# A planned attention and two-layer MLP kernel: more buffers at the start of the first batch, fewer warm-up matmuls, and the second batch's k and q sums moved from accumulating DMAs to VectorE

## The chip, the cores and the metric

One NeuronCore of one Trainium2 chip runs the whole program. The metric is the time of the program on the device in microseconds (us). It is the median of three runs; one further run, made with the hardware profiler, gives the trace.

## The reference, cut to what matters

Attention over 4 batches, 8 heads, 576 positions and 64 channels, then two feed-forward layers over 2304 tokens (512 to 2048 to 512 features). Attention is a sum of two parts: one on k, q and v averaged over groups of four positions, one local with a band of seven positions.

```python
q_d = q.reshape(B, H, Sd, factor, D).mean(axis=3)      # factor = 4, Sd = 144
k_d = k.reshape(B, H, Sd, factor, D).mean(axis=3)
v_d = v.reshape(B, H, Sd, factor, D).mean(axis=3)
out_up = np.repeat(sm_attn(q_d, k_d, v_d), factor, axis=2)
mask = np.abs(pos[:, None] - pos[None, :]) < factor
scores = np.where(mask, scale * np.matmul(q, k.transpose(0, 1, 3, 2)), -1e9)
x = out_up + softmax(scores) @ v                       # then heads beside each other: [2304, 512]
h = x @ moe_w_in;  x = (h * sigmoid(h)) @ moe_w_out
h = x @ moe2_w_in; g = P(h) / (Q(h) + 1e-6);  out = g @ moe2_w_out
```

## The kernel before

All matrix products of the two layers are made of three products each of high and low parts (fp32r), so a layer step is 24 matmuls: 12 for the first product (`h`, L807) and 12 for the second (`o`, L821). The first layer walks over five blocks of tokens (480 or 384) and 16 slices of the hidden width, 80 steps in all. The first block takes 8 steps, the second block 16, then the first block's other 8, then the rest.

The order of the work is not written out by hand. `Plan` (L94) keeps a list of jobs; each has a cost in ns for every engine that may do it (P is TensorE, V VectorE, A ScalarE, G GpSimd, D the SyncE DMA queue), jobs that must be done before it, and slots of rings (buffers) that it takes and gives back. `run` (L122) goes through the planned time and gives each job to an engine; `settle` (L112) repeats it and keeps the best. The result is one fixed order of instructions for each engine, and each engine's queue runs in that order. A job with `port` that V or G may do goes to the first free one of "VG" (L194), and such jobs do not overlap in the plan.

One attention job chain per batch `b`:

- `L` loads k and q of a third of the positions into a `kq` buffer (ring of 4). `v` and `V` load v.
- Sums of four positions: for batch 0 the jobs `R` make them on VectorE from the loaded `kq` (L408), and the jobs `p` make those of v on GpSimd or VectorE (L424, L426, L427). For the later batches the jobs `K` and `Q` load four slices with DMAs, three of them accumulating DMAs that GpSimd issues (L437, L444).
- Averaged part, two halves `m`: scores `s` (L471), maximum `m`, exponent `e` (ACT, L487), sum `u`, normalising `n` (L496, one job of 864 columns), transposes `t` (L505), copies `c`, product `o` (L519), copy `U` to `up`.
- Local part, six chunks `c` of 96 tokens: scores `S` (L572, L581), `M` (L587), `E` (L597), `U` (L602), `N` (L606), transposes `T` (L617), copy `C`, product `O` (L637), then `A` adds the two parts into `xs` (L644, ring of 2), `H` copies the high part, `X` subtracts it for the low part (L659).

Chunks 0 to 4 of batch 0 make the first block of tokens, so the first `h` step waits for these five. Weights are converted on the chip: each slice of a weight matrix is one `piece` of seven jobs on ACT, VectorE and GpSimd (L719 to L743), ahead of the step that uses it.

While TensorE has nothing to do it is kept busy with matmuls on a constant (`warm`, L287). They write the PSUM tile `wps`, which has the tag `h` and so one of the two buffers of the `h` steps; a tile keeps its buffer up to its last use in the program. `warm(20)` stands in front, and gaps in the plan are filled up to a planned time of `HEAD + 15000` ns (L1011 to L1015).

Of the kernel before, what the change touches and what calls it, by code (L numbers as in the profile page):

```python
# [21 lines left out]
CH = 96  # L22
# [29 lines left out]
EARLY = 50000.0  # L52
ROUNDS = 6
WARM0 = 20
WARM_SHARE = 0.8

# [37 lines left out]
class Plan:  # L94
# [27 lines left out]
    def run(self, when):  # L122
# [26 lines left out]
        while events:  # L149
# [18 lines left out]
            while again:  # L168
                again = False
                for j in pool:  # L170
# [22 lines left out]
                    if "G" in j.cost and "V" in j.cost and j.port:  # L193
                        best = next((e for e in "VG" if free[e] <= t), None)  # L194
                        if best is None:
                            continue
# [58 lines left out]
def tile_kernel(ctx, tc, kq, kqs, vp, vw_in, moe_w_in, moe_w_out, moe2_w_in, moe2_w_out, moe2_a, moe2_b, out):  # L255
# [119 lines left out]
    def attention(b):  # L375
# [22 lines left out]
        if b == 0:  # L398
            for t in range(3):
                for w in range(2):  # L400
                    def sm(e, t=t, w=w):
                        if w == 0:
                            o = kd[:, :, SUB * t:SUB * t + SUB]
                            i = kqt[t][:, :KT * KW].rearrange("p (g s) -> p g s", g=KT)[:, :, HALO:HALO + TH]
                        else:
                            o = qd[:, :KT * SD].rearrange("p (g s) -> p g s", g=KT)[:, :, SUB * t:SUB * t + SUB]
                            i = kqt[t][:, KT * KW:KT * (KW + TH)].rearrange("p (g s) -> p g s", g=KT)
                        nc.vector.tensor_reduce(out=o, in_=i.rearrange("p g (j r) -> p g j r", r=4), axis=AX.X, op=ALU.add)  # L408
                    sums.append(plan.add(f"R{b}{t}{w}", FAR, {"V": v_ns(768)}, sm, after=[loads[t]] + sums[:1],
                                         take=[] if sums else [kdu], give=[kqu[t]]))  # L410
            for i in range(2):
                for hf in range(2):
# [16 lines left out]
                    vs.append(plan.add(f"p{b}{i}{hf}", FAR, {"G": 2050, "V": 1950}, pv,  # L429
                                       after=[l] + vs[:1], take=[] if vs else [vdu], give=[u]))  # L430
        else:
# [14 lines left out]
            for f, u, o, n, m in ((ks, kdu, sums, "K", 128 * 4608), (vsum, vdu, vs, "Q", HS * 4096)):  # L446
                j = None
                for r in range(4):
                    j = plan.add(f"{n}{b}{r}", FAR, {"G": 1000} if r else {"D": 60}, lambda e, f=f, r=r: f(e, r),
                                 after=[j] if j else takes[n], take=[] if j else [u], size=m, margin=500 if r else 0)  # L450
                    if r == 0:
                        takes[n] = [j]
                o.append(j)
        if b == 0:
            takes.update(K=sums[:1], Q=vs[:1])

# [3 lines left out]
        for m in range(2):  # L460
# [34 lines left out]
            def no(e, x=x):  # L495
                eng(e).tensor_tensor(out=x["e"][:, :, :SD], in0=x["e"][:, :, :SD],  # L496
                                     in1=x["r"].unsqueeze(2).to_broadcast([128, 6, SD]), op=ALU.mult)
# [34 lines left out]
            jn = plan.add(f"n{b}{m}", d0, {"V": v_ns(864), "G": 130 + 1.9 * 864}, no, after=[ju], port=True)  # L532
            pc, pt_ = [], []
            for e_, u in ((0, p1_), (1, p2)):
                jt = plan.add(f"t{b}{m}{e_}", d0, {"P": 500}, lambda e, tr=tr, e_=e_, u=u: tr(e, e_=e_, u=u),
                              after=[jn] + pt_[:1], take=[u] + ([pt] if e_ == 0 else []), give=[eu], margin=MARGIN if b else MARGIN0)
# [9 lines left out]
        for c in range(NCH):  # L546
# [7 lines left out]
            wn = NF - 3 + c // 2  # L554
            if b == 0 and c in (3, 4):
                pt = v0u.setdefault("PT", Unit("w8"))
# [84 lines left out]
            def ad(e, x=x, c=c):  # L641
                x["x"] = at.tile([128, KT, CH], F32, tag="xs", name="xs", bufs=2)
# [18 lines left out]
            if i == 0:  # L661
# [14 lines left out]
            jo = plan.add(f"O{b}{c}", d0, {"P": 700}, pv, after=[jc, jl] + ups, take=[pO, xu], give=[pt, vu],  # L676
                          margin=MARGIN if b else MARGIN0)
            ja = plan.add(f"A{b}{c}", d0, {"V": 2 * v_ns(192)}, ad, after=[jo], give=[pO, upu])
# [331 lines left out]
    busy = 0.0  # L1010
# [173 lines left out]
```

## Time and profile before

| what | value |
| --- | --- |
| three runs, median | 925.39 us |
| three runs, range | 923.1 to 926.2 us |
| profiled execution, its own time | 925.37 us |
| profiled execution, span from first to last instruction | 923.6 us |
| TensorE matmul busy | 906.2 us (98%) |
| TensorE weight loads busy | 762.3 us (83%) |
| VectorE busy | 711.4 us (77%) |
| ScalarE busy | 606.8 us (66%) |
| GpSimd busy | 333.2 us (36%) |
| mean granted TensorE clock | 0.996 |

The profiled execution took as long as the median of the runs, and 1.8 us of its time lie outside the span. Times of rows below count from the start of the span. The chain of work that ended last runs through TensorE for 91% of the span. An average says little here: attention of the first batch, attention beside the first layer, and the two layers alone follow each other, and only the first 112 us hold waits of TensorE.

### The profile page before, as it was taken

How to read it: one execution, taken by the hardware profiler on the slowest of the kernel's cores; microseconds unless marked ns; L12 is line 12 of the kernel's file. 1: busy time of each engine (PE TensorE's matmuls, PEld its weight loads, DVE VectorE, ACT ScalarE, POOL GpSimd, SP SyncE). 2: the span in 40 equal slices, each digit the busy share in tenths (PEclk: the TensorE clock that was granted, in tenths of full speed). 3: DMA queues.
4: the chain of work that ended last, by engine and by line, in shares of the span. 5: the costliest groups of instructions: out<-in, count | busy, mean ns of one | idle time of the engine just before them, and what ended most of it. 6: DMA issues, size and time to landing. Idle time of an engine off the chain costs nothing.

```text
span 923.6 us, 16216 instructions
## 1 busy us (share of the span) xinstructions
PE 906.2 (98%) x6212; PEld 762.3 (83%) x6212; DVE 711.4 (77%) x1060; ACT 606.8 (66%) x1224; POOL 333.2 (36%) x279
## 2 busy tenths in 40 slices
PE   8988999999999999999999999999999999999997
PEld 6766788877887778878899988888888888999996
DVE  6979876996557876785332399998998999799995
ACT  4957655786446764674322488877877777787874
POOL 4534240142022410121000155655555555455553
PEclk9989999999999999999999999999999999999999
DMA  9878997779789777779685091002001000200000
GB/s 282 287 217 247 277 282 279 251 268 301 220 269 294 238 276 276 268 245 363 213 288 210 5 392 48 1 1 92 1 1 48 33 1 1 80 1 0 35 1 35
DMA packets 48042, 153.03 MB, mean 166 GB/s; under 512 B 5244, under 2 KB 10492, under 8 KB 47964
## 3 DMA queue, kind: packets, MB, share of 16 engines
q1 hardware_dynamic: 44972, 143.03, 44.1%
q0 software_dynamic: 2704, 8.95, 5.4%
q8 instruction: 49, 0.80, 0.4%
q14 instruction: 29, 0.24, 0.1%
q10 hardware_dynamic: 288, 0.00, 0.0%
HBM read 116.38 MB, written 35.59 MB: 165 GB/s over the span
## 4 chain that ended last, share of the span: by engine, by line
PE 91%; DVE 4%; ACT 3%; issue 1%; POOL 0%; ACTq 0%; DVEq 0%; POOLq 0%
PE hps L807 43%; PE acc L1054 21%; PE acc L821 21%; PE wps L289 1%; PE pair L637 1%; PE pair L581 1%; PE pair L519 1%; ACT E L597 1%; PE pair L617 1%; DVE cw L735 1%; ACT cr L723 0%; DVE cr L732 0%; ACT PT L332 0%; DVE cw L728 0%; PE pair L471 0%
## 5 line engine op out<-in xcount | busy, mean ns | idle before, releaser
L807 PE MATMUL hps<-xh,w 128*128 128x480 f32 (+1 forms) x640 | 226.0, 381 | 3.6 <-DVE th L973 3.0
L821 PE MATMUL acc<-gh,wo 128*128 128x480 f32 (+1 forms) x640 | 222.8, 376 | 0.0
L807 PE MATMUL hps<-x2h,wi 128*128 128x512 f32 (+1 forms) x640 | 196.4, 368 | 0.0
L894 POOL TENSOR_TENSOR u<-u,ah 128x512 f32<-128x512 f32 (+1 forms) x80 | 96.0, 1200 | 262.7 <-ACT u L892 261.1
L1054 PE MATMUL acc<-wo,gh 128*128 128x512 f32 x576 | 178.0, 390 | 0.0
L807 PEld LDWEIGHTS hps<-xh,w 128*128 128x128 f32 x640 | 121.1, 189 | 22.5 <-DVE th L973 3.8
L821 PEld LDWEIGHTS acc<-gh,wo 128*128 128x128 f32 x640 | 119.8, 188 | 17.4 <-issue 1.8
L807 PEld LDWEIGHTS hps<-x2h,wi 128*128 128x128 f32 x640 | 118.8, 188 | 16.3
L1085 POOL TENSOR_TENSOR gl<-p,gh 128x512 fp32r<-128x512 f32 (+1 forms) x80 | 121.2, 1515 | 11.6 <-issue 8.9
L1054 PEld LDWEIGHTS acc<-wo,gh 128*128 128x128 f32 x576 | 107.6, 188 | 20.9
L807 PE MATMUL hps<-xl,w 128*128 128x480 f32 (+1 forms) x320 | 120.0, 375 | 1.1 <-DVE xl L659 1.0
L821 PE MATMUL acc<-gl,wo 128*128 128x480 f32 (+1 forms) x320 | 118.6, 371 | 0.4 <-POOL gl L982 0.4
L807 PE MATMUL hps<-x2l,wi 128*128 128x512 f32 (+1 forms) x320 | 117.7, 368 | 0.0
L1054 PE MATMUL acc<-wo,gl 128*128 128x512 f32 x288 | 112.7, 391 | 0.0
L970 ACT ACTIVATE th<-hps 128x480 f32<-128x480 f32 (+1 forms) x80 | 44.5, 557 | 101.7 <-PE hps L807 100.8
L973 DVE SCALAR_TENSOR_TENSOR th<-th,hps 128x480 f32<-128x480 f32 (+1 forms) x80 | 50.4, 631 | 78.9 <-ACT th L970 78.5
L1077 DVE SCALAR_TENSOR_TENSOR u<-u,r 128x512 f32<-128x512 f32 (+1 forms) x80 | 100.1, 1252 | 2.8
L1070 ACT ACTIVATE r<-u,cst 128x512 f32<-128x512 f32 (+1 forms) x80 | 54.5, 682 | 52.7 <-POOL u L894 52.7
L1076 DVE SCALAR_TENSOR_TENSOR u<-u,r 128x512 f32<-128x512 f32 (+1 forms) x80 | 82.7, 1034 | 0.5 <-ACT r L1071 0.5
L732 POOL TENSOR_TENSOR cr<-cw,cr 128x512 int32<-128x512 int32 x22 | 30.9, 1407 | 135.0 <-DVE cw L728 86.2
L891 DVE TENSOR_TENSOR p<-p,hps 128x512 f32<-128x512 f32 (+1 forms) x80 | 50.5, 631 | 31.5 <-ACT p L890 31.3
L332 ACT ACTIVATE gh<-th 128x480 fp32r<-128x480 f32 (+1 forms) x80 | 47.4, 592 | 31.8 <-DVE th L973 28.5
(123 smaller groups left out, 1485.4 us busy)
## 6 DMA issues: line engine op xcount, KB each, us to landing
wo<-wos SPq DMA_DIRECT2D x64, 512.0 KB, 5.8
raw<-moe_w_in SPq DMA_DIRECT2D x32, 512.0 KB, 5.0
raw<-moe_w_out SPq DMA_DIRECT2D x32, 512.0 KB, 5.9
w2s<-cvo SPq DMA_DIRECT2D x32, 512.0 KB, 5.2
kq<-kq SPq DMA_DIRECT2D x12, 788.0 KB, 7.5
wos<-wo SPq DMA_DIRECT2D x16, 512.0 KB, 3.1
wi<-w2s SPq DMA_DIRECT2D x16, 512.0 KB, 6.6
wo<-w2s SPq DMA_DIRECT2D x16, 512.0 KB, 9.7
```

The lines of the kernel that those rows point to most:

```text
L332: nc.scalar.activation(out, in_, AF.Copy, scale=scale)
L807: nc.tensor.matmul(hps[:, :n], lhsT=wi[:, i, 128 * g:128 * g + 128], rhs=(a, b)[s][:, g, :n], start=(m == 0), stop=(m == len(mms) - 1))
L821: nc.tensor.matmul(acc_t[p][g // 2][:, g % 2, :n], lhsT=wo[:, i, 128 * g:128 * g + 128], rhs=s_[:, :n], start=(f == f0 and m % 3 == 0), st ...
L891: nc.vector.tensor_tensor(out=p, in0=p, in1=hps, op=ALU.mult)
L894: nc.gpsimd.tensor_tensor(out=u, in0=u, in1=ah, op=ALU.mult)
L970: nc.scalar.activation(x["t"][:, :n], x["h"][:, :n], AF.Tanh, scale=0.5)
L973: nc.vector.scalar_tensor_tensor(out=x["t"][:, :n], in0=x["t"][:, :n], scalar=1.0, in1=x["h"][:, :n], op0=ALU.add, op1=ALU.mult)
L1054: nc.tensor.matmul(acc2[j][c], lhsT=a[:, 128 * c:128 * c + 128], rhs=wo[:, i, :], start=(f == 0 and m % 3 == 0), stop=(f == NF - 1 and m % ...
L1070: nc.scalar.activation(r, u, AF.Ln, scale=2.0 ** -64, bias=cst[:, 0:1])
L1076: nc.vector.scalar_tensor_tensor(out=u, in0=u, scalar=1.000001, in1=r, op0=ALU.add, op1=ALU.mult)
L1077: nc.vector.scalar_tensor_tensor(out=u, in0=u, scalar=-2.0, in1=r, op0=ALU.add, op1=ALU.mult)
L1085: nc.gpsimd.tensor_tensor(out=gl2[k_][:, :n], in0=p, in1=gh2[k_][:, :n], op=ALU.subtract)
```

## The change

Seven edits. (1) The four chunks 2 to 5 of batch 0 get `xs` buffers in the weight slots w9 and w10, one slot for two chunks; the product `O` of chunks 3 and 5 takes no slot of its own and follows the product before it. (2) The sums of v in batch 0 may run on GpSimd alone. (3) A `port` job that GpSimd or VectorE may do prefers GpSimd when another job that only VectorE can do, and that is no `port` job, is ready. (4) `n` is two jobs of 432 columns each, and the transposes of a half wait for their own half. (5) Batch 1's sums of k and q are made like batch 0's, by the six `R` jobs on VectorE from the loaded `kq`; its `K` jobs and their four DMAs are gone. (6) The take-over of the sum buffers from batch to batch follows this. (7) The fill-up with warm-up matmuls counts from 3500 ns on.

```diff
+SUMS_V = 2
+COLD = 3500.0
@@ Plan.run
                     if "G" in j.cost and "V" in j.cost and j.port:
-                        best = next((e for e in "VG" if free[e] <= t), None)
+                        rest = any(x.ready <= t and not x.port and x.only() == "V" for x in pool)
+                        best = next((e for e in ("GV" if rest else "VG") if free[e] <= t), None)
@@ attention
-        if b == 0:
+        if b < SUMS_V:
             for t in range(3):
                 for w in range(2):
...
+        if b == 0:
             for i in range(2):
...
-                    vs.append(plan.add(f"p{b}{i}{hf}", FAR, {"G": 2050, "V": 1950}, pv,
+                    vs.append(plan.add(f"p{b}{i}{hf}", FAR, {"G": 2050}, pv,
...
+                if n == "K" and b < SUMS_V:
+                    continue
...
-                                 after=[j] if j else takes[n], take=[] if j else [u], size=m, margin=500 if r else 0)
+                                 after=[j] if j else takes[n] if b > 1 or n == "Q" else [], take=[] if j else [u], size=m, margin=500 if r else 0)
...
+        elif b < SUMS_V:
+            takes.update(K=sums[:1])
...
-                eng(e).tensor_tensor(out=x["e"][:, :, :SD], in0=x["e"][:, :, :SD],
-                                     in1=x["r"].unsqueeze(2).to_broadcast([128, 6, SD]), op=ALU.mult)
+                i = slice(3 * e_, 3 * e_ + 3)
+                eng(e).tensor_tensor(out=x["e"][:, i, :SD], in0=x["e"][:, i, :SD],
+                                     in1=x["r"][:, i].unsqueeze(2).to_broadcast([128, 3, SD]), op=ALU.mult)
...
-            jn = plan.add(f"n{b}{m}", d0, {"V": v_ns(864), "G": 130 + 1.9 * 864}, no, after=[ju], port=True)
+            jn = [plan.add(f"n{b}{m}{e_}", d0, {"V": v_ns(432), "G": 130 + 1.9 * 432}, lambda e, no=no, e_=e_: no(e, e_=e_),
+                           after=[ju], port=True) for e_ in range(2)]
...
-                              after=[jn] + pt_[:1], take=[u] + ([pt] if e_ == 0 else []), give=[eu], margin=MARGIN if b else MARGIN0)
+                              after=[jn[e_]] + pt_[:1], take=[u] + ([pt] if e_ == 0 else []), give=[eu], margin=MARGIN if b else MARGIN0)
...
+            if b == 0 and c >= 2:
+                xu = v0u.setdefault(("xs", c // 2), Unit(f"w{NF - 8 + c // 2}"))
...
+                if b == 0 and c >= 2:
+                    if c % 2 == 0:
+                        v0t["xs", c // 2] = wp.tile([128, 2, KT, CH], F32, tag=f"w{NF - 8 + c // 2}", name="xs2")
+                    x["x"] = v0t["xs", c // 2][:, c % 2]
...
-            jo = plan.add(f"O{b}{c}", d0, {"P": 700}, pv, after=[jc, jl] + ups, take=[pO, xu], give=[pt, vu],
+            jo = plan.add(f"O{b}{c}", d0, {"P": 700}, pv, after=[jc, jl] + ups + (o2 if b == 0 and c in (3, 5) else []), take=[pO] + ([] if b == 0 and c in (3, 5) else [xu]), give=[pt, vu],
                           margin=MARGIN if b else MARGIN0)
+            o2 = [jo]
@@ the fill-up
-    busy = 0.0
+    busy = COLD
```

## Rows read from the trace of the kernel before

**Rows 1.** Windows: start:end, length, busy us (count) per engine, PEclk, DMA share, GB/s
```profile
14.00:29.00 15.00, 12.32 (x251) 9.44 (x248) 13.91 (x25) 12.94 (x54) 12.79 (x12) 1.00 1.02 364
29.00:45.00 16.00, 14.83 (x393) 11.31 (x387) 15.20 (x36) 15.06 (x46) 7.56 (x7) 1.00 0.81 242
45.00:60.00 15.00, 11.02 (x84) 8.44 (x77) 10.42 (x22) 6.80 (x19) 7.03 (x7) 0.77 0.95 263
56.00:60.00 4.00, 4.00 (x18) 2.85 (x18) 0.18 (x1) 0.76 (x2) 1.27 (x2) 0.50 1.05 242
...
60.00:112.00 52.00, 48.95 (x480) 37.19 (x478) 47.03 (x82) 37.78 (x84) 16.83 (x14) 1.00 0.81 242
```
**Rows 2.** Waits of TensorE from 100 us to the end: total, times, longest
```profile
PE hps L807 <- ACT xh L332: 0.4, 1, 0.4
```
**Rows 3.** Timeline: start us, length us, engine, line, operation, count, [idle before <-releaser]; the start
```profile
1.06 8.71 PE L289 MATMUL wps<-wz 128*128 128x256 bf16 x59 [1.06 <-DVE wz L284]
6.73 1.81 DVE L408 TENSOR_REDUCE kqd<-kq 128x192 f32<-128x768 f32 x2 [2.39 <-DMA kq<-kq]
10.63 0.61 DVE L587 TENSOR_REDUCE n<-pair 128x8 f32<-128x432 f32 x1 [2.09 <-PE pair L581]
```
**Rows 4.** Timeline from the first exponent to the averaged part's result
```profile
19.14 0.21 ACT L593 ACTIVATE n<-n 128x8 f32<-128x8 f32 x1 [1.71 <-DVE n L587]
20.23 1.98 DVE L424 TENSOR_REDUCE vd<-vst 72x256 f32<-72x1024 f32 x1
25.22 3.39 POOL L496 TENSOR_TENSOR EE<-EE,r 128x864 f32<-128x864 f32 x2 [0.21 <-ACT EE L487]
34.69 0.41 ACT L332 ACTIVATE up<-pair 128x288 f32<-128x288 f32 x1
```
**Rows 5.** Timeline from the first local product to the first layer's first step
```profile
35.34 0.68 PE L637 MATMUL pair<-PT,vw 54*64 54x48 f32 x32
40.11 0.61 DVE L644 TENSOR_TENSOR xs<-acc,up 128x192 f32<-128x192 f32 x2
42.89 1.03 DVE L659 TENSOR_TENSOR xl<-xs,xh 128x384 fp32r<-128x384 f32 x2
45.77 1.52 DVE L732 CUSTOM_DVE_ANT_0 cr<-cw,cr 128x1024 uint16<-128x1024 uint16 x1
48.34 0.48 PE L807 MATMUL hps<-xl,w 128*128 128x480 f32 x1 [0.97 <-DVE xl L659]
```
**Rows 6.** Timeline of TensorE in the second step and after it
```profile
54.01 0.77 PE L807 MATMUL hps<-xh,w 128*128 128x480 f32 x1 [3.01 <-DVE th L973]
57.37 1.00 PE L807 MATMUL hps<-xh,w 128*128 128x480 f32 x2
59.70 1.39 PE L289 MATMUL wps<-wz 128*128 128x256 bf16 x10
63.24 0.59 PE L807 MATMUL hps<-xh,w 128*128 128x480 f32 x2
```
**Rows 7.** Groups by line: count, busy us, mean ns, idle before: the sums, and their DMAs' issue
```profile
L408 DVE TENSOR_REDUCE kqd<-kq 128x192 f32<-128x768 f32 x6 | 5.4, 945 | 2.4 <-DMA kq<-kq 2.4
L437 POOL DMA_DIRECT2D kqd<-kqs x9 | 8.8, 974 | 0.7 <-DMA kqd<-kqs 0.7
```
**Rows 8.** Timeline: VectorE's idle time behind the second step
```profile
59.82 0.65 DVE L973 SCALAR_TENSOR_TENSOR th<-th,hps 128x480 f32<-128x480 f32 x1 [4.34 <-ACT th L970]
```
**Rows 9.** Timeline: VectorE beside GpSimd
```profile
60.39 0.68 DVE L743 TENSOR_TENSOR w<-cw,w 128x512 fp32r<-128x512 f32 x1
66.84 1.30 POOL L743 TENSOR_TENSOR wo<-cw,wo 128x512 fp32r<-128x512 f32 x1 [9.57 <-ACT wo L332]
67.36 1.33 DVE L743 TENSOR_TENSOR w<-cw,w 128x512 fp32r<-128x512 f32 x1
70.17 0.61 DVE L602 TENSOR_REDUCE r<-E 128x8 f32<-128x440 f32 x1
70.20 1.29 POOL L732 TENSOR_TENSOR cr<-cw,cr 128x512 int32<-128x512 int32 x1 [2.06 <-ACT E L597]
```

More of the change, by code (lines that the diff above doesn't have):

```diff
@@ L493, in su, with no @@
                 nc.vector.reciprocal(out=x["r"], in_=x["r"])
-            def no(e, x=x):
-                eng(e).tensor_tensor(out=x["e"][:, :, :SD], in0=x["e"][:, :, :SD],
-                                     in1=x["r"].unsqueeze(2).to_broadcast([128, 6, SD]), op=ALU.mult)
+            def no(e, x=x, e_=0):
+                i = slice(3 * e_, 3 * e_ + 3)
+                eng(e).tensor_tensor(out=x["e"][:, i, :SD], in0=x["e"][:, i, :SD],
+                                     in1=x["r"][:, i].unsqueeze(2).to_broadcast([128, 3, SD]), op=ALU.mult)
             def tr(e, x=x, e_=0, u=None):
@@ L641, in ad @@
             def ad(e, x=x, c=c):
-                x["x"] = at.tile([128, KT, CH], F32, tag="xs", name="xs", bufs=2)
+                if b == 0 and c >= 2:
+                    if c % 2 == 0:
+                        v0t["xs", c // 2] = wp.tile([128, 2, KT, CH], F32, tag=f"w{NF - 8 + c // 2}", name="xs2")
+                    x["x"] = v0t["xs", c // 2][:, c % 2]
+                else:
+                    x["x"] = at.tile([128, KT, CH], F32, tag="xs", name="xs", bufs=2)
                 for a in range(2):
```

## The prediction

> **What bounds the kernel now.** I read the busy times by stretch first, then TensorE's waits, then the head instruction by instruction. From 60 us on TensorE is busy for 48.95 of 52 us [rows 1], and from 100 us to the end it waits 0.4 us in all [rows 2]. Everything behind 112 us is a queue of TensorE work that the change leaves as long as it is; what moves is when that queue starts and what TensorE loses before it is dense. The head has three stages. Up to 10.6 us TensorE runs 59 warm-up matmuls [rows 3]. From there to 34.7 us ScalarE is the tight engine: 12.94 of 15 us, then 15.06 of 16 [rows 1], with one idle stretch of 1.71 us [rows 4]. From 35.3 to 48.3 us the chunks are added up and split, while VectorE is busy 15.20 of 16 us [rows 1, 5]. [...]
>
> **The change part by part.**
>
> *Warm-up.* 59 matmuls are 20 plus 39, so the plan's first TensorE job starts between 39 x 109 / 0.8 = 5314 and 5450 ns. Counting from 3500 leaves (1814 to 1950) x 0.8 / 109 = 13 or 14, in all 33 or 34. At 8.71 / 59 = 0.148 us each they end at 1.06 + 34 x 0.148 = 6.1 us, a little later if the first ones are the slow ones, and still before the first k and q land, which let VectorE start at 6.73 [rows 3]. The first scores then start at about 6.8 instead of behind the warm-up at 9.8, and end before VectorE has done its two sums at 8.54. The first maximum moves from 10.63 to about 8.55: the 2.09 us that VectorE waited for TensorE [rows 3]. Nothing is late in its place before the second and third loads; those were not waited for before, so at 2 us less they cost between 0 and 2 us. I take 0.
>
> *From there to `up`.* ScalarE is nearly full, so a gain here is at most the start's 2.1 plus its idle 1.71 [rows 4]. The v sum of 1.98 us on VectorE goes; its GpSimd twin is planned at 2.05 in the kernel's text, on an engine that is busy 12.79 of 15 us [rows 1, 4]. VectorE's gain lies under ScalarE's work, and GpSimd's 2.05 lies ahead of the two normalisations, 3.39 us back to back [rows 4]. Halved, the first transposes need a quarter of these, 0.85 us, instead of half, which gives back 0.85. Bounds for this stage: 0.5 us (2.1 less 2.05, plus 0.45 of the half) and 3.8. I take 2.5, near the shift of the start, because ScalarE's row says that little else can be pulled ahead.
>
> *Buffers.* From the first local product at 35.34 to the matmul that reads the last low part at 48.34 are 13.0 us [rows 5]. With two `xs` buffers the third chunk's sum starts only at 40.11. Without that wait VectorE needs 5 x 0.61 us of sums (two instructions took 0.61) and 5 x 0.51 of subtractions (two took 1.03) [rows 5], 5.6 us; with the first product, one high-part copy and the hand-overs, an estimate of three times the product's 0.68 [rows 5], 2.0 us, it is a floor of 7.6. The gain is 5.4 if nothing else runs between, and 0 if weight conversions such as the 1.52 us one at 45.77 still fill the stretch. I take 3.0, a little over half: the wait itself goes, but the second step's weights are still converted here. The slots w9 and w10 are asked for again only by slices 9 and 10, whose step stands behind 17 others, so that cover is long; if it failed, a load of weights would wait, not TensorE.
>
> *k and q sums of batch 1.* Six reductions of 0.945 us, 5.67 us, are added to VectorE, and four DMAs of 576 KB fall away, three with a GpSimd issue of 0.97 us each [rows 7]: 2.36 MB, at the 242 to 364 GB/s of the head [rows 1] 6 to 10 us of transfer time. Batch 1's third `kq` load has to come earlier for it, 0.79 MB on the SyncE queue, with its turn before weight loads. Cover on VectorE: 4.34 us idle behind the second step [rows 8] and about 5 of 52 us after 60 [rows 1]. Queued behind the sums are batch 1's maxima and weight conversions, and TensorE waits for both. The price is 0 to 5.7 us; I take 1.0, since the idle time is 9 us, most of it right where the sums fall, and GpSimd takes over some conversions.
>
> *GpSimd first.* A job moved costs GpSimd about 1.3 us where VectorE needs 0.68 [rows 9]; GpSimd is free two thirds of the time after 60 us [rows 1]. It pays when VectorE meanwhile does what it was chosen for. A reduction beside a GpSimd job took 0.61 us, no longer than alone; a two-input conversion took 1.33 instead of 0.68 [rows 9]. So the pairing that the rule looks for is the good one, but order on the chip drifts from the plan. Between -3 and +5 us; I take -1.0, nearer to the reduction's row, because the six new sums are such reductions.
>
> [...]
>
> *The second step.* It waits for the first step's activation on VectorE, although the ring has two buffers, because warm-up matmuls still run at 59.70 and hold one [rows 6]. [...] The change touches neither; I take 0, bounds -5.4 and +5.4 (a step less or a step more).
>
> Sum: -2.5 - 3.0 + 1.0 - 1.0 = -5.5 us. The profiled execution took 925.37 us, 1.8 of it outside the span of 923.6, and equals the median of 925.39; so 920 us.
>
> **The rivals.**
>
> *One bank for longer (no change).* The limit of the warm-up is a planned time, 49 us. If the plan starts the first layer earlier, more steps lie before that limit, and a gap of 0.14 us in the plan is enough for a warm-up that holds the buffer. One more step that waits for its forerunner's activation costs 3.0 + 2.4 = 5.4 us: 920 + 5.4 = 925. For it: a planned start 3 us earlier is half a step. Against it: other TensorE work can fill such a wait, and the plan has a gap only where weights are late.
>
> *VectorE becomes the bound (slower).* Place: 45 to 112 us, where VectorE is busy 57.4 of 67 us [rows 1]; 9.6 idle. The sums take 5.7. If ten jobs that moved to GpSimd each stretch a conversion by 0.65 us (1.33 less 0.68), 6.5 more; together 12.2 against 9.6. Two more us are lost because the head's 5.5 us earlier start shortens the stretch for the same conversions: that eats the head's gain and leaves 12.2 - 9.6 + 2 = 4.6 us on top: 930. It decides once more than about six moved jobs overlap conversions. Against: moved jobs also take 0.68 each off VectorE, 6.8 for ten.
>
> *The head's gains add up and the second step's wait goes too (more gain).* All upper bounds, with the sums at 1: 2.1 + 1.7 + 5.4 + 5.4 - 1 = 13.6: 912.
>
> *The change doesn't do what it says.* If weights set the first steps, an earlier first block only waits longer: 924 to 926, told with the first rival.
>
> **How the numbers follow.** The forecast (gain of 3 to 9 us) has 0.54, the double gain 0.09, no change by the first or the last rival 0.21, slower 0.16. About 0.3%, 2.8 us, is what a measurement of this kernel can tell from no change: faster is below 922.6. Faster 0.63, same 0.21, slower 0.16. The forecast's own range is 916 to 922.5. The range for 8 in 10 is 913 to 929: it takes in the unchanged case and the near half of the slower one, and leaves out the far ends, about 0.14.
>
> **What would show it.** In the changed profile: 33 or 34 warm-up matmuls in front and the first scores near 6.8; the first maximum near 8.5; `up` near 32; the third chunk's sum right behind the second; the first low-part matmul near 43; the second step's wait and clock as before; the six sums between 25 and 70 us at 0.94 each; TensorE dense by 106. I am wrong if the first layer starts near 43 but TensorE then waits for weights or batch 1's maxima (the sums or GpSimd), if steps wait for the activation of the one before more than once (the bank), or if `up` stays near 35 (GpSimd ahead of the normalisations).

## The result and the profile after

The changed kernel takes 936.85 us (median of four runs) against 924.92 us of the kernel before: ratio 1.0107, 95% interval 1.0076 to 1.0137. It is slower by 12 us by the medians, against a forecast of 920.0 and a range of 913 to 929. The ratio takes in all four runs: three took 936.7 to 937.2 us and one 928.66. The profiled execution took 936.97 us with a span of 935.2, 11.6 more than before. The second layer starts 10.2 us later than before (529.08 instead of 518.84 us), so nearly all of the loss lies in front of it. Lines have moved: L293 is the old L289, L412 the old L408, L480 the old L471, L506 the old L496, L662 the old L644, L762 the old L743, L826 and L840 the old L807 and L821.

Windows of the changed kernel: start:end, length, busy us (count) of PE, PEld, DVE, ACT, POOL, then PEclk, DMA share, GB/s.

```profile
29.00:45.00 16.00, 14.84 (x281) 11.71 (x284) 10.35 (x23) 8.06 (x17) 6.19 (x6) 0.50 0.58 210
45.00:60.00 15.00, 14.08 (x178) 10.93 (x174) 13.22 (x22) 12.44 (x43) 8.33 (x7) 0.93 0.61 196
60.00:112.00 52.00, 45.73 (x473) 34.53 (x472) 44.01 (x85) 35.20 (x81) 17.93 (x15) 0.87 0.72 224
...
27.00:47.00 20.00, 18.37 (x346) 14.30 (x350) 13.40 (x27) 10.78 (x26) 6.19 (x6) 0.50 0.65 242
```

Against [rows 1] three things differ. From 29 to 45 us the granted clock is 0.50 where it was 1.00: TensorE is as busy as before (14.84 and 14.83 us) with 281 matmuls instead of 393, and ScalarE and VectorE, which wait for it (3.1 us for L529 and 5.1 for L650), are idle for half and a third of the stretch. The last window shows the whole of it, 20 us at 0.50. From 45 to 112 us VectorE is busy 57.2 of 67 us; before it was 57.4 (the six sums lie ahead of this stretch). And from 60 to 112 us TensorE does a little less than before, at a mean clock of 0.87.

Where TensorE's time went can be read from four more windows, from the start to the first matmul of the second layer: the kernel before and the changed one, then TensorE's warm-up matmuls alone in both.

```profile
0.00:518.84 518.84, 506.61 (x4364) 420.70 (x4365) 355.82 (x641) 298.29 (x709) 119.28 (x119) 0.99 0.80 260
0.00:529.08 529.08, 513.02 (x4338) 426.06 (x4339) 366.16 (x650) 296.49 (x707) 122.10 (x124) 0.97 0.75 251
...
0.00:518.84 518.84, 25.15 (x180) 0.99 0.80 260
0.00:529.08 529.08, 22.81 (x154) 0.97 0.75 251
```

Both kernels run the same 4,184 matmuls of their own there. Without the warm-ups these keep TensorE busy for 481.5 us before and 490.2 in the changed kernel, 8.7 us longer, while idle time and warm-ups together, the time in which TensorE waits, grow by 1.5 us only (37.4 to 38.9). So most of the loss in front of the second layer is the same work taking longer. The granted clock is at 0.50 from 26.7 to 47.2, from 67.7 to 77.9 and from 84.8 to 88.2 us, 34 us in all; before it was so for 6.8 us (53.2 to 60.0).

Timeline of the changed kernel: start us, length us, engine, line, operation, count, [idle before <-releaser].

```profile
1.06 6.30 PE L293 MATMUL wps<-wz 128*128 128x256 bf16 x33 [1.06 <-DVE wz L288]
7.20 0.35 PE L585 MATMUL pair<-bands,ident 128*128 128x216 bf16 x2
8.50 0.60 DVE L600 TENSOR_REDUCE n<-pair 128x8 f32<-128x432 f32 x1
...
23.34 4.50 DVE L506 TENSOR_TENSOR EE<-EE,r 128x432 f32<-128x432 f32 x2
23.36 1.77 POOL L506 TENSOR_TENSOR EE<-EE,r 128x432 f32<-128x432 f32 x2
25.09 1.77 POOL L619 TENSOR_TENSOR E<-E,r 128x432 f32<-128x432 f32 x2
27.47 0.70 PE L515 MATMUL pair<-ident,EE 48*72 48x48 f32 x12 [2.49 <-DVE EE L506]
35.12 0.41 ACT L336 ACTIVATE up<-acc 128x288 f32<-128x288 f32 x1 [1.63 <-PE acc L529]
38.95 0.62 DVE L662 TENSOR_TENSOR xs<-acc,up 128x192 f32<-128x192 f32 x2 [0.16 <-PE acc L650]
39.49 0.94 DVE L412 TENSOR_REDUCE kqd<-kq 128x192 f32<-128x768 f32 x1
48.50 0.47 PE L826 MATMUL hps<-xh,w 128*128 128x480 f32 x1
52.84 0.96 PE L480 MATMUL pair<-kqd 64*64 64x144 f32 x24
58.37 0.97 PE L480 MATMUL pair<-kqd 64*64 64x144 f32 x24 [0.59 <-ACT EE L496]
70.71 0.69 DVE L762 TENSOR_TENSOR w<-cw,w 128x512 fp32r<-128x512 f32 x1
73.47 0.77 PE L826 MATMUL hps<-xh,w 128*128 128x480 f32 x1
```

Read it from above. The start does what it should: 33 warm-ups, first maximum at 8.50 instead of 10.63 [rows 3]. At 23.3 us four GpSimd jobs lie beside two VectorE normalisations, which take 4.50 us; TensorE waits 2.49 us for them, and from 26.7 us on its clock is low. `up` is complete at 35.5 us, 0.4 later than before [rows 4]. The sums into `xs` follow each other with only a k sum between, so the buffers are there, but they start at 38 us. The last rows are another change: batch 1's scores of the averaged part (L480), which ran at 73.0 and 77.8 us before, now run at 52.8 and 58.4, and the last weight conversion in front of the third step (L762) ends only at 71.4 us, where the one at 60.39 ended at 61.1 before [rows 9]. The third step starts at 73.47 instead of 62.81. In the kernel before (timeline):

```profile
62.81 0.38 PE L807 MATMUL hps<-xh,w 128*128 128x480 f32 x1
73.00 0.97 PE L471 MATMUL pair<-kqd 64*64 64x144 f32 x24
```

The weights were late before these scores ran. The second step's conversion ended at 44.5 us before and at 57.2 in the changed kernel, and the third step's weights, the third load of `moe_w_in`, were asked for at 35.91 instead of 21.59 us, while batch 1's k and q loads (three by 19.5 us) stand in front of them in the SyncE queue. Timeline of the kernel before, then of the changed one:

```profile
21.59 0.43 SPq L711 DMA_DIRECT2D raw<-moe_w_in  x1
43.84 0.68 DVE L743 TENSOR_TENSOR w<-cw,w 128x512 fp32r<-128x512 f32 x1
...
12.35 0.33 SPq L396 DMA_DIRECT2D kq<-kq  x1
19.03 0.80 SPq L396 DMA_DIRECT2D kq<-kq  x2
35.91 0.43 SPq L730 DMA_DIRECT2D raw<-moe_w_in  x1
55.96 1.28 POOL L762 TENSOR_TENSOR w<-cw,w 128x512 fp32r<-128x512 f32 x1
```

Waits of TensorE in the changed kernel behind 112 us (total us, times, longest), where the kernel before had one of 0.4 [rows 2]:

```profile
PE acc L1073 <- POOL gl L1104: 1.6, 1, 1.6
PE acc L840 <- DVE xe L334: 0.7, 1, 0.7
PE hps L826 <- POOL w L762: 0.7, 1, 0.7
```

With two more of 0.2 us these are 3.4 us, a further and smaller loss.

### The profile page after: what moved, and what is told of

Same layout as the page of the kernel before. It is cut to its first block, busy times and chain, and to the rows that moved or that the text cites. A ratio compares the mean times of both kernels' runs of the same rounds, so it can differ in the third digit from the quotient of the medians.

```text
span 935.2 us, 16162 instructions
## 1 busy us (share of the span) xinstructions
PE 912.9 (98%) x6186; PEld 767.7 (82%) x6186; DVE 720.8 (77%) x1069; ACT 604.7 (65%) x1222; POOL 335.7 (36%) x284
## 4 chain that ended last, share of the span: by engine, by line
PE 87%; DVE 6%; issue 2%; ACT 2%; POOL 1%; DMA 1%; ACTq 0%; DVEq 0%; POOLq 0%
PE hps L826 40%; PE acc L1073 21%; PE acc L840 19%; PE pair L650 1%; PE pair L594 1%; DVE cw L754 1%; PE wps L293 1%; PE pair L630 1%; ACT EE L496 1%; DVE EE L506 1%; PE pair L529 1%; PE pair L515 1%; ACT E L610 1%; DVE r L615 0%; DVE cw L747 0%
## 5 line engine op out<-in xcount | busy, mean ns | idle before, releaser
L826 PE MATMUL hps<-xh,w 128*128 128x480 f32 (+1 forms) x640 | 225.6, 382 | 1.0 <-POOL w L762 1.0
L840 PE MATMUL acc<-gh,wo 128*128 128x480 f32 (+1 forms) x640 | 221.6, 377 | 0.7 <-DVE xe L334 0.7
L826 PE MATMUL hps<-x2h,wi 128*128 128x512 f32 (+1 forms) x640 | 196.4, 368 | 0.0
L826 PEld LDWEIGHTS hps<-xh,w 128*128 128x128 f32 x640 | 121.0, 189 | 19.4 <-POOL w L762 1.8
L840 PEld LDWEIGHTS acc<-gh,wo 128*128 128x128 f32 x640 | 120.1, 188 | 18.0 <-DVE xe L334 1.1
L826 PEld LDWEIGHTS hps<-x2h,wi 128*128 128x128 f32 x640 | 118.9, 188 | 16.3
L1104 POOL TENSOR_TENSOR gl<-p,gh 128x512 fp32r<-128x512 f32 (+1 forms) x80 | 120.8, 1510 | 11.6 <-issue 8.8
L826 PE MATMUL hps<-xl,w 128*128 128x480 f32 (+1 forms) x320 | 120.1, 375 | 0.0
L840 PE MATMUL acc<-gl,wo 128*128 128x480 f32 (+1 forms) x320 | 118.8, 371 | 0.0
L826 PE MATMUL hps<-x2l,wi 128*128 128x512 f32 (+1 forms) x320 | 117.7, 368 | 0.0
L1001 DVE TENSOR_TENSOR gl<-th,gh 128x480 fp32r<-128x480 f32 (+1 forms) x73 | 51.3, 704 | 27.5 <-ACT gh L336 27.4
## 6 DMA issues: line engine op xcount, KB each, us to landing
wi<-w2s SPq DMA_DIRECT2D x16, 512.0 KB, 10.2
```

The costliest lines, as they stand in the source:

```text
L826: nc.tensor.matmul(hps[:, :n], lhsT=wi[:, i, 128 * g:128 * g + 128], rhs=(a, b)[s][:, g, :n], start=(m == 0), stop=(m == len(mms) - 1))
L840: nc.tensor.matmul(acc_t[p][g // 2][:, g % 2, :n], lhsT=wo[:, i, 128 * g:128 * g + 128], rhs=s_[:, :n], start=(f == f0 and m % 3 == 0), st ...
L1001: eng(e).tensor_tensor(out=gl_t[s][:, :n], in0=x["t"][:, :n], in1=gh_t[s][:, :n], op=ALU.subtract)
L1104: nc.gpsimd.tensor_tensor(out=gl2[k_][:, :n], in0=p, in1=gh2[k_][:, :n], op=ALU.subtract)
```

## The experiments

Two theories stood against each other. "Clock": the collision at 23 us makes TensorE wait, the clock falls, and 20 us at half speed are the loss. "Sums": batch 1's sums on VectorE cost the time, by VectorE's work or by the order of loads and jobs that they bring. Ratios are against the kernel before, with their 95% intervals; differences in us are between medians.

**The wait filled with warm-ups.** After, with 24 warm-up matmuls in front of the first transposes.

```diff
     for x in order:
         if x.eng == "P":
...
+        if x.name == "t001":
+            warm(24)
         x.emit(x.eng)
```

> The changed kernel with 24 more warm-up matmuls in front of the transposes that waited 2.49 us for the normalisation on VectorE; every other instruction and its order unchanged. Theory 'clock': the wait itself is short, but the granted clock falls to 0.50 behind it for 20.2 us; with TensorE fed in the wait the clock stays at 1.00 from 27 to 47 us, the first step starts 4 to 8 us earlier and the time falls by 6 to 9 us, to 928 to 931. Theory 'weights': the first steps wait for the converted weights anyway, whose order is the same; then the clock stays up but the time falls by less than 3 us, above 934.

930.84 us, 1.0063 (1.0048 to 1.0078): 6.0 us less than after, as the clock theory's size has it. In its timeline the VectorE pair is as slow as in after (4.42 us), and a longer gap of 3.50 us has come, in which TensorE waits for nothing that the timeline names (the last section takes it up):

```profile
43.33 0.20 PE L594 MATMUL pair<-kq 64*64 64x54 f32 x1 [3.50 <-issue]
```

In its windows the clock is at 0.91 where after had 0.50:

```profile
27.00:47.00 20.00, 15.41 (x380) 11.81 (x379) 16.09 (x33) 15.02 (x46) 7.47 (x7) 0.91 0.81 286
```

So holding the clock there gives back 6 us and not 12: in front of the second layer TensorE's own work is 9.0 us shorter than in after, and the fill and the gap make its waiting 2.2 us longer. The one run of after whose mean granted clock was 0.992 instead of 0.981 took 928.66 us, 2 us less than the filled kernel.

**All thin stretches filled.** The same at six places.

```diff
+        warm({"t001": 24, "t100": 8, "T05": 3, "t101": 5, "O05": 6, "t110": 10}.get(x.name, 0))
```

> The same, and 32 more warm-up matmuls in the five waits of 0.4 to 1.3 us between 63 and 71 us, behind which the clock was at 0.50 for 10.1 us. Theory 'clock': another 3 to 5 us below the kernel that fills the first wait alone, since TensorE has 7 us of layer work in that stretch. Theory 'weights': no gain beyond 1 us, since the steps behind are set by their weights.

930.35 us (five runs, 927.56 to 933.18), 1.0058 (1.0035 to 1.0081), no more than the first fill. In the profiled execution, the fastest of the five, the mean granted clock is 0.997 as before (0.996), the first step starts at 43.2 us, 3.7 earlier than before, and still the third starts late in the timeline:

```profile
67.33 0.48 PE L826 MATMUL hps<-xh,w 128*128 128x480 f32 x1
```

The median is 5.7 us above the kernel before, but it belongs to a run at 0.994; the profiled execution, with the clock held, took 927.56 us, 2.2 more than that of the kernel before. So 2 to 6 us are left that the clock doesn't explain.

**The collision taken apart.** After, with the normalisations `N` of chunks 2 and 3 on VectorE, so that only two GpSimd jobs lie beside the halves.

```diff
-        x.emit(x.eng)
+        x.emit({"N02": "V", "N03": "V"}.get(x.name, x.eng))
```

> The changed kernel with two normalisations of the local part (chunks 2 and 3) issued on VectorE instead of GpSimd, at the same place in the order, so that GpSimd has two jobs in a row instead of four beside VectorE's two half normalisations. [...] Rival: the two halves are slow by themselves (broadcast operand) and still take over 4 us; time as the changed kernel, 937.

Beside two GpSimd jobs instead of four the two halves were expected at about 2.7 us instead of 4.50, with TensorE's wait under 1.2 us, no low clock behind it, and the time of the first filled kernel within 2 us.

933.44 us, 1.0092 (1.0077 to 1.0107), 3.4 us less than after. Its timeline and, below, TensorE's wait:

```profile
23.38 2.78 DVE L506 TENSOR_TENSOR EE<-EE,r 128x432 f32<-128x432 f32 x2
```

```profile
PE pair L515 <- DVE EE L506: 0.8, 1, 0.8
```

The same two instructions take 2.78 instead of 4.50 us and TensorE's wait falls from 2.49 to 0.8: GpSimd's jobs did stretch VectorE's. The other half of the expectation failed: the clock still fell for 17 us, from 26 to 37 and from 40 to 47. Removing the long wait is not enough. The clock fell as well in two kernels below, with the sums by DMA and with the scores held back, where TensorE's longest wait at this place is 0.6 and 1.0 us; what lets it fall there stays open.

**Batch 1's sums by DMA again.** After with only edit 5 undone, and 6, which follows it.

```diff
-SUMS_V = 2
+SUMS_V = 1
```

> The changed kernel with batch 1's k and q sums made by accumulating DMAs as before. Theory 'sums': the six sums on VectorE and the three early k and q loads that go in front of weight loads delay the weights of steps 1 to 3; without them the third step starts near 62 us instead of 73 and the time is at or below the kernel before, 918 to 926. Theory 'clock alone': the order of the halves and of GpSimd stays as bad, the clock falls all the same and the time stays above 930.

927.11 us, 1.0027 (1.0017 to 1.0038): 9.7 us less than after. That is most of the loss, but not the gain that the rest was to bring. The plan is a new one as a whole: the third load of `moe_w_in` goes out at 20.48 us again, and GpSimd has three jobs of the averaged part in a row at 22.3 us, with no VectorE pair beside them. The clock is at 0.50 for 13.7 us here too (28 to 42 us), and the third step is early again in its timeline:

```profile
57.78 0.48 PE L826 MATMUL hps<-xh,w 128*128 128x480 f32 x1
```

**The sums' work taken off, their place kept.** All thin stretches filled, and each of batch 1's six sums replaced by a copy of every fourth element. In the traces the six take 2.9 us of VectorE instead of 5.5.

```diff
+                        if b:
+                            nc.vector.tensor_copy(o, i[:, :, :, 0])
+                        else:
+                            nc.vector.tensor_reduce(out=o, in_=i, axis=AX.X, op=ALU.add)
```

> The kernel with both waits filled, in which batch 1's six sums are replaced by copies of every fourth element (the sum over four positions is left out there, so batch 1's averaged part is computed from other numbers). Order and transfers unchanged; VectorE has about 6 x 0.6 = 3.6 us less to do. Theory 'VectorE is the bound': the time falls by 2 to 4 us against the filled kernel's 930.4. Theory 'order': the work that stands in front of the weights is the same, and the time changes by less than 1.5 us.

929.0 us, 1.0039 (1.0026 to 1.0051), 1.35 less than with the whole sums, with intervals that overlap, and the third step starts at 68.65 us, no earlier than with them. VectorE's time for the sums is not the price. Loads and order are as in after, so this run doesn't tell these two apart.

**The sums kept, the order of before.** After, with batch 1's averaged scores held back in the plan until the weight piece `I2` is converted.

```diff
+    by = {x.name: x for x in plan.jobs}
+    by["s10"].after.append(by["I2.7"])
+    by["s11"].after.append(by["I2.7"])
     order = plan.settle(guess, ROUNDS)
```

> The changed kernel, sums on VectorE, in which batch 1's averaged scores may start in the plan only when slice 2 of the first weights is converted; the plan then puts these scores 13 us later and the third step earlier. Theory 'order': sums that are ready early let batch 1's averaged part go in front of the weight conversions; held back, the third step starts near 62 us instead of 74 and the time falls to 925 to 930 with VectorE doing as much as in the changed kernel. Theory 'VectorE is the bound': no gain beyond what the clock gives, 933 or more.

924.53 us (ten runs), 0.9988 (0.9972 to 1.0004): 12.3 us less than after, with all sums on VectorE. Timeline and windows:

```profile
58.21 0.68 DVE L762 TENSOR_TENSOR w<-cw,w 128x512 fp32r<-128x512 f32 x1
...
59.39 0.38 PE L826 MATMUL hps<-xh,w 128*128 128x480 f32 x1
```

```profile
27.00:47.00 20.00, 19.94 (x380) 16.04 (x375) 16.48 (x37) 13.93 (x43) 9.55 (x9) 0.66 0.79 281
...
45.00:60.00 15.00, 14.27 (x84) 11.60 (x82) 14.38 (x26) 10.46 (x27) 7.14 (x7) 1.00 0.75 212
...
60.00:112.00 52.00, 46.70 (x525) 35.09 (x525) 46.99 (x87) 38.07 (x90) 17.23 (x13) 0.97 0.62 208
```

The conversion ends at 58.9 instead of 71.4 us and the third step starts 14 us earlier. VectorE is busy 61.4 of 67 us from 45 to 112, 4 more than in the slower kernel, two of the six sums among them. From 27 to 47 us the clock is still at 0.66 on average, and yet the kernel takes as long as before. Holding the scores back makes a new plan as a whole, not one moved job. The work is the same, but three things changed besides the scores: the third load of `moe_w_in` goes out at 20.02 us instead of 35.91, the last two sums run only at 48.8 and 50.7 us, and TensorE's wait for the normalisations is 1.0 us instead of 2.49. So this run shows that an order exists in which the sums on VectorE cost nothing against the kernel before; it doesn't show that the scores alone make the difference. No run moved the loads alone. From its timeline:

```profile
20.02 0.33 SPq L730 DMA_DIRECT2D raw<-moe_w_in  x1
```

**The warm-up alone.** The kernel before with edit 7 only.

```diff
-    busy = 0.0
+    busy = 3500.0
```

> The kernel before with the fill-up counted from 3500 ns, nothing else: 33 or 34 warm-up matmuls in front instead of 59, all other instructions in the same order. Theory of the prediction: the start moves 2 us and the rest of the head follows, 922.5 to 924. Rival 'cover': the first step is set by what runs between, the gain is under 1 us; or the clock falls in the thinner stretch and the time rises to 927 or more.

922.64 us, 0.9972 (0.9959 to 0.9985), a gain of 2.6. The route is not the expected one: the first step starts at 47.78 us, 0.9 later than before, but the third at 58.53 instead of 62.81. The gain shows in the second step, which waits 1.64 us instead of 3.01 and runs at full clock (a pair of matmuls takes 0.60 us, 1.00 before [rows 6]). The second step in the timeline:

```profile
52.36 0.48 PE L807 MATMUL hps<-xh,w 128*128 128x480 f32 x1 [1.64 <-DVE th L973]
```

**The bank set free.** That kernel, without warm-ups behind the start of the first step.

```diff
     for x in order:
+        if x.name == "h0.1":
+            HOLD.append(1)
         if x.eng == "P":
-            if busy < HEAD + 15000:
+            if busy < HEAD + 15000 and not HOLD:
```

> The kernel before with the fill-up counted from 3500 ns (922.6 us alone) and no warm-up matmul behind the first step; all other instructions in the same order. Theory 'bank': the ten warm-up matmuls behind the second step hold one of the two PSUM buffers; without them the second step no longer waits for the first step's activation (1.6 us of wait there) and starts right behind the first, and the time falls by 1 to 3 us more, to 920 to 921.5. Rival: the second or third step's weights are ready no earlier (near 61 us in the kernel before), so the wait moves to the third step and the time stays within 1 us of 922.6.

920.08 us, 0.9936 (0.9915 to 0.9958): 2.6 less again, the fastest kernel of the study, faster than both. The first and second step in the timeline (one row for the matmuls between, which repeat):

```profile
44.75 0.46 PE L807 MATMUL hps<-xh,w 128*128 128x480 f32 x1
46.58 0.49 PE L807 MATMUL hps<-xl,w 128*128 128x480 f32 x1 [1.37 <-DVE xl L659]
46.91 0.59 PE L807 MATMUL hps<-xh,w 128*128 128x480 f32 x2
...
51.49 0.38 PE L807 MATMUL hps<-xh,w 128*128 128x480 f32 x1
```

The two steps follow each other without a gap, and the wait for L973, 3.0 us before [rows 6], is gone, as the reading has it that the warm-ups' tile holds one of the two buffers. How much of the 2.6 us is the buffer's is not settled: the first step starts 3.0 us earlier than with the warm-up alone, although TensorE's instructions are the same up to there; that kernel's trace has a gap of 1.89 us marked "issue" in front of it and a low clock from 44.5 to 47.9 us, and this one's has neither.

**The buffers.** The kernel before with edits 7 and 1.

```diff
-                x["x"] = at.tile([128, KT, CH], F32, tag="xs", name="xs", bufs=2)
+                if b == 0 and c >= 2:
+                    if c % 2 == 0:
+                        v0t["xs", c // 2] = wp.tile([128, 2, KT, CH], F32, tag=f"w{NF - 8 + c // 2}", name="xs2")
+                    x["x"] = v0t["xs", c // 2][:, c % 2]
...
```

> The kernel before with the fill-up counted from 3500 ns and the four more buffers for the sums of chunks 2 to 5, none of the other edits. Theory of the prediction: the buffers take 3 us off the head: 919.5 to 921. Rival 'weights': the first two steps start earlier but the third does not, since its weights set it: 922 to 925.

924.96 us, 0.9998 (0.9971 to 1.0026; ten runs from 921 to 933). The profiled execution, the fastest of the ten at 921.13 us:

```profile
39.65 0.46 PE L815 MATMUL hps<-xh,w 128*128 128x480 f32 x1
56.22 0.48 PE L815 MATMUL hps<-xh,w 128*128 128x480 f32 x1
```

The first step starts 8.1 us earlier than with the warm-up alone (5.1 earlier than in the trace of the freed bank, which has no gap in front of it), the third 2.3 us earlier (56.22, was 58.53). The median shows no gain over the warm-up alone, and the fastest run 1.5 us. The ten runs go with their mean granted clock, from 0.997 in the fastest to 0.981 in the slowest; why the same program gets a different clock from run to run is not settled.

**GpSimd first.** The kernel before with edits 7 and 3.

```diff
-                        best = next((e for e in "VG" if free[e] <= t), None)
+                        rest = any(x.ready <= t and not x.port and x.only() == "V" for x in pool)
+                        best = next((e for e in ("GV" if rest else "VG") if free[e] <= t), None)
```

> The kernel before with the fill-up counted from 3500 ns and the rule that prefers GpSimd when VectorE has other work, none of the other edits. [...] Rival (the prediction's): the rule relieves VectorE, 920 to 922.

924.52 us, 0.9991 (0.9976 to 1.0007), within the 924 to 928 expected if more GpSimd jobs lie beside two-input VectorE jobs and stretch them; 1.9 above the warm-up alone by the medians, though the two intervals overlap. The rule brings no gain that can be seen.

**Two more fills, on the kernel with the sums by DMA.** First 39 warm-ups spread over ten places, to hold the clock from 28 to 42 us; then the same with every warm-up of the kernel replaced by half as many of twice the columns.

```diff
+        warm({"t001": 6, "T02": 3, "o00": 4, "T03": 3, "T04": 3, "o01": 6, "S05": 5, "O00": 3, "O02": 3, "O03": 3}.get(x.name, 0))
```

> The changed kernel with batch 1's sums by DMA again, and 39 more warm-up matmuls spread over the stretch from 25 to 36 us behind which its clock was at 0.50 for 13.7 us. Theory 'clock and sums': without both the edits that remain (buffers, fewer warm-ups at the start, halves) keep their gain: the first step starts near 41 us, the clock stays at 1.00 up to 60 us, and the time is 920 to 924, below the kernel before. Rival 'weights set the pace': the first step starts earlier but the third still near 57.8, and the time stays at 926 to 928.

929.16 us, 1.0036 (1.0023 to 1.005), 2.1 above the kernel without the fill, although the clock is at 1.00 up to 45 us. The first step waits behind a gap of 3.10 us marked "issue". No expectation held. Nor does the third step's start alone set the time: here it starts at 59.98 us, 7.4 earlier than in the changed kernel with all thin stretches filled, and the median is only 1.2 us lower, with intervals that overlap.

```diff
-        for _ in range(n):
-            nc.tensor.matmul(wps[:, :256], lhsT=wz, rhs=wz.unsqueeze(1).to_broadcast([128, 2, 128]), start=True, stop=True)
+        for _ in range((n + 1) // 2):
+            nc.tensor.matmul(wps, lhsT=wz, rhs=wz.unsqueeze(1).to_broadcast([128, 4, 128]), start=True, stop=True)
```

> The kernel with batch 1's sums by DMA and the thin stretch filled (929.2 us), with all warm-up matmuls of 512 columns and half as many. TensorE waited 3.10 us there for nothing that the trace names, behind 1460 matmuls and weight loads; five kernels had such a wait of 0.6 to 3.6 us at that same count and two at 1206, 255 before. Theory 'instruction supply': the wait belongs to the instruction count, where the next piece of TensorE's program has to be fetched; with some 180 instructions less in front it is met later, behind the start of the first step, the first step starts near 44 us instead of 47.7 and the time falls by 1 to 3 us. Rival: it is a hidden wait for data and stays at the same work, near 44 us.

931.28 us, 1.006 (1.0042 to 1.0078): no gain from the shorter count. The gap did not go; it moved to other work, behind another count of instructions (window up to its end, then the timeline):

```profile
0.00:42.80 42.80, 37.07 (x602) 20.00 (x602) 29.39 (x60) 26.17 (x90) 22.48 (x40) 1.00 0.90 286
```

```profile
42.81 0.37 PE L650 MATMUL pair<-PT2c,vw 54*64 54x48 f32 x9 [2.45 <-issue]
```

## Why the prediction was wrong, point by point

*Warm-up: right at the start, the gain by luck.* 33 matmuls, first scores at 7.20 (6.8 forecast), first maximum at 8.50 (8.55). Alone the edit is worth 2.6 us, near the 2.5 taken for the start and the way to `up` together. But the first step came no earlier for it; the gain came in the second step, where the prediction had put 0.

*Up to `up`: wrong.* `up` near 32 was forecast; it came at 35.5. The text had named this as a sign against it ("GpSimd ahead of the normalisations"), and that is what the trace shows: the start's 2.1 us are lost at 23 us. ScalarE, taken for the tight engine, is busy 8.06 of 16 us behind that wait. The prediction's own rows had VectorE busier than ScalarE in both stretches, 13.91 of 15 and 15.20 of 16 us [rows 1], so VectorE's jobs in front of TensorE were the ones to watch.

*Buffers: the mechanism right, the 3.0 us not.* Alone they bring the first step 5 to 8 us forward, as much as the bound of 5.4 or more, and the median shows none of it. The fourth rival had said why: weights set the next steps. It stood at part of 0.21 and should have been weighed for this term, whose own text says that the second step's weights are still converted in that stretch. In the changed kernel the first step isn't even earlier (48.5 us, 46.9 before); with the clock held it starts at 45.4 and, with all fills, at 43.2.

*k and q sums: the step that failed.* "The price is 0 to 5.7 us; I take 1.0" counts VectorE's time against VectorE's idle time. The size of that count was sound, but it was the wrong count: taking half of the work away gives back 1.35 us at most. Nor does the idle time lie where the sums fall: the six ran between 27.8 and 42.7 us, the idle time at 55.5 to 59.8 and behind 60 [rows 8, 1]. The price is 9.7 us, measured by undoing the edit. What the prediction named and put at nothing is the order: batch 1's third k and q load comes "with its turn before weight loads". In the changed kernel three such loads go out by 19.5 us and the third step's weights are asked for 14.3 us later than before; with the edit undone, and with the scores held back, they go out at 20 us and the time comes back. The other candidate is that sums which are ready early let batch 1's scores, and what follows from them, run from 52.8 us on, while the conversions that the third step needs wait on VectorE. The weights were late before that, so the scores can't be the whole cause; the two were never moved one by one, and which one costs how much stays open.

*GpSimd first: the wrong place.* The bounds of -3 to +5 were worked out from conversions behind 60 us [rows 9]. The collision lies at 23 us. The rows that the prediction had, 1.33 instead of 0.68 us [rows 9], already told that a GpSimd job stretches a two-input VectorE job; that four such jobs in a row could stand in front of TensorE's next work, and that the clock would follow, was missed. Half of them taken away gives back 3.4 us, the clock held there 6.0; how much of that is the rule's and how much the split and the v sums' is not separated. What the runs show of the stretch are the two VectorE normalisations: 4.50 us beside four GpSimd jobs, 2.78 beside two.

*The second step: not as said.* It was left at 0, as a wait and a clock that the change doesn't touch. The 3.0 + 2.4 = 5.4 us of the bounds and of the first rival are the wait of 3.01 us and an estimate from [rows 6]: twelve matmuls at a granted clock of 0.50, six pairs at 1.00 instead of 0.59 us. In the changed kernel both the wait and the low clock are gone: no wait for the activation is left there and the clock is 1.00 from 48 to 60 us. But the step starts at 56.28 us, 2.3 later than before, with batch 1's first scores in front of it and its weights finished only at 57.2.

*The rivals.* The one on the slower side had the sign and not the mechanism: VectorE did not become the bound (57.2 of 67 us; the kernel with held scores, which is faster, has 61.4). An order that makes the weights late, by loads or by jobs in front of them, was in none of the cases, nor was a lower clock, so none gave more than 930.

*The parts.* The profiled executions can be taken apart as in the first section: the time that TensorE waits in front of the second layer (idle or on warm-ups), its own 4,184 matmuls there, and everything behind (us).

| kernel | waits in front | own work in front | behind | span |
| --- | --- | --- | --- | --- |
| before | 37.4 | 481.5 | 404.7 | 923.6 |
| changed | 38.9 | 490.2 | 406.1 | 935.2 |
| first fill | 41.1 | 481.2 | 406.1 | 928.5 |
| sums by DMA | 33.4 | 486.9 | 404.7 | 925.1 |
| scores held back | 34.3 | 486.3 | 404.5 | 925.1 |

Against the kernel before, the changed one loses 8.7 us by slower work, 1.5 by waiting and 1.4 behind. Against the two kernels in which the weights go out early it loses 5 us by waiting, 3 to 4 by slower work (the clock is at 0.50 for 17 us there up to 112 us, instead of 34) and 1.5 behind. So the price of the sums and the price of the clock overlap and are not a sum: undoing the edit brings the weights early and halves the time at the low clock as well. The late waits of 3.4 us were not tried by themselves; with the scores held back the only ones behind 112 us are 1.9 and 0.2.

## What to carry to other kernels

In a kernel whose order a list planner makes, an input that is wanted earlier is not free: its loads, and the work that it makes ready, can go in front of what the next step needs. So ask which loads and jobs it will overtake, and look at the last load, conversion or copy ahead of the next step, not at the engine's idle share. Look for engines that stretch each other's jobs where a short run of such jobs stands in front of TensorE: here two VectorE jobs took 4.50 us beside four of GpSimd and 2.78 beside two, and a wait of 2.5 us was followed by 20 us at half clock. Split TensorE's time into waiting and own work before you name a cause: a busy engine at half clock looks full (14.84 of 16 us with 281 matmuls at 0.50, 14.83 with 393 at 1.00). An earlier first step was worth at most 1.5 us here while the next steps' inputs stayed where they were; keeping warm-ups out from behind the first step's start was worth 2.6 us for a few lines.

## What was not expected of the hardware

Between 36 and 45 us gaps of TensorE marked "issue" lie at the same two counts of its instructions in most of the kernels. In the kernel before and in seven of the others one lies behind some 1,460 matmuls and weight loads (1,459 before, 1,461 with the first fill); in the changed kernel and two others one lies behind some 1,205 (1,206 in the changed one, 1,204 with the longer warm-ups), that is 255 earlier. Three kernels have neither, and elsewhere gaps so marked, up to 1.3 us, lie at other counts. Windows from the start to the end of the gap, first the kernel before (gap 0.56 us):

```profile
0.00:43.29 43.29, 38.39 (x729) 29.64 (x730) 33.68 (x71) 30.64 (x111) 23.58 (x39) 1.00 0.88 281
```

then the kernel with the first fill (gap 3.50 us):

```profile
0.00:43.32 43.32, 35.36 (x730) 27.62 (x731) 33.44 (x62) 28.89 (x102) 22.45 (x40) 1.00 0.87 293
```

In the same kernel the DMA queues of 39.9 to 43.3 us and, as the last row, of the whole program (packets, MB, share of the 16 engines):

```profile
q1 hardware_dynamic: 508, 1.33, 100.8%
q8 instruction: 1, 0.02, 2.0%
...
q8 instruction: 49, 0.80, 0.4%
```

The last row has 49 packets of 16 KB, one for each 253 of its 12,400 or so matmuls and weight loads, which is near the spacing of 255. From these numbers and the queue's name the estimate is that it brings TensorE's instructions. One such packet is moved while TensorE stands still and data fill the 16 engines to 100.8%. That TensorE waits for this packet is suggested and not shown: when it was asked for can't be seen, nor why most others are not waited for; the warm-up alone has a gap of 1.89 us at this count and the kernel with the freed bank, whose instructions are the same up to there, has none. It could explain a part of what extra warm-ups cost: in the filled kernel with the sums by DMA, and in both fills of the changed kernel, the gap was 3.1 to 3.5 us, where it was 0.17 and 1.16 us without. But it was 2.42 us, with no fill, where two normalisations went to VectorE, so the warm-ups are not what makes it long by themselves.
